# Linear attention and a feed-forward layer on one core: chunks of 384 tokens for 256, TensorE's order pinned, weights decoded without GpSimd

## The chip, the core and the metric

The kernel runs on one core of a Trainium2 chip. The metric is the time of one execution in microseconds (us) on the device; a comparison takes the median of several executions. Five engines work side by side, each through its own instructions in order: TensorE (PE, with its weight loads shown as PEld), VectorE (DVE), ScalarE (ACT), GpSimd (POOL) and SyncE (SP), which here issues the DMA transfers. They meet at semaphores. PE writes into PSUM, which has eight banks of 512 float32 for each of 128 partitions.

## What is computed

```python
def phi(x):                                   # M = 128 random features
    proj = np.einsum('bhsd,md->bhsm', x, omega)
    h = proj - np.sum(x * x, axis=-1, keepdims=True) / 2.0
    h = h - np.max(h, axis=-1, keepdims=True)
    return np.exp(h) / np.sqrt(m)
q_p, k_p = phi(q * scale), phi(k * scale)
kv = np.einsum('bhsm,bhsd->bhmd', k_p, v)
z = np.sum(k_p, axis=2)
num = np.einsum('bhsm,bhmd->bhsd', q_p, kv)
den = np.einsum('bhsm,bhm->bhs', q_p, z)[..., None] + 1e-06
x = (num / den).transpose(0, 2, 1, 3).reshape(B * S, H * D)
h = x @ w_in
out = (h - np.tanh(h)) @ w_out
```

B = 8 batches, H = 8 heads, S = 576 tokens, D = 64; so x has 4608 rows (tokens) of 512. w_in is 512 x 2048 and w_out 2048 x 512. The inputs q, k, v and omega are float32; **both weight matrices arrive as float64**, as pairs of 32-bit words, and the kernel itself turns them into float32.

## The kernel before

**Products.** A float32 product is done on PE in one of two ways. *Native*: one matmul of float32 operands as they are. *Single-pass*: each operand is split into hi (rounded to the type float32r) and lo = x - hi, and the three products hi·hi, hi·lo and lo·hi are added up in PSUM. The feed-forward is single-pass throughout: three matmuls for one.

**Attention.** It works in units of two heads (a head pair, c = 0 to 3). A unit of keys (`k_unit` L156, then `k_single` L202) forms the features of one batch, sums kv (`pk`) and z and spreads z over the partitions (`zb`). A unit of queries (`q_unit` L291) takes 256 tokens: features (L118 single-pass, or `features_f` L139 native with its reductions at L148 and exponentials at L150), denominators on DVE (L322), reciprocal (L325), scaling (L329 on ACT, L331 on DVE or POOL), transposes (L338), numerators (L346 native, L362 and L363 single-pass), and the split into `xh` and `xl`. Each unit is a generator: every `yield` ends a stage, and `tick` (L482) moves all open units by one stage.

**Decoding.** `decode` (L384) takes half a slice of weights (512 words for each partition, 256 for the last four slices) from float64 to hi and lo: ACT L398 and L408, POOL L399 and L409, DVE L400, L402, L405 and L406, and one addition (L410) by turns on POOL and DVE. There are 16 slices of d_ff, each with its part of w_in and of w_out.

**Feed-forward.** Tokens go in 18 chunks of 256. A step takes two slices of d_ff. `ffn_h` (L421) does 24 matmuls 256 wide (L428) into one bank, by turns `h0` and `h1`; ACT takes the tanh (L432), DVE subtracts it from h (L433), ACT rounds to `gh` (L434), and L435 forms `gl`. `ffn_out` (L438) does 12 matmuls 512 wide into `po0` and `po1` (L445 to L447), one step behind, and `ffn_store` (L449) copies out a finished chunk.

**Order of work.** At the start, the keys of batch 0 and the queries of chunks 0 and 1 go natively, while the first weights come. Then, for each of eight steps, two slices are decoded and chunks 0 and 1 are worked off with them (loop at L527), with the native keys of batch 1 and queries of chunks 2 and 3 between. From then on one chunk at a time is done with all weights in SBUF, and a table of start times (L572 to L581) lets a query unit start every four half steps and a key unit where its batch is needed. A scheduler then orders the instructions of every engine by its own estimates, PE's too.

## Time and profile before

| | |
|---|---|
| median of 3 executions | 1107.24 us (1106.55 to 1107.78) |
| span of the profiled execution | 1105.4 us |
| PE, PEld | 1063.0 us (96%), 966.1 us (87%) |
| DVE | 900.0 us (81%) |
| ACT | 703.7 us (64%) |
| POOL | 403.1 us (36%) |
| HBM read, written | 45.15 MB, 9.44 MB |

The profile is that of one execution. The page gives the busy time of each engine over the span; queries of the trace give the same for stretches of time, for groups of equal instructions (count, busy time, mean duration of one, and what ended the idle time before them), and for single instructions in order of time. Matmuls are pipelined: the duration of one overlaps the next, so what a matmul costs is read from start to start.

### The profile page before, as it was taken

Reading aid. Unit: us, or ns where it says so; the run is one execution under the profiler, and the core shown is the slowest. Engines: PE = TensorE matmul, PEld = TensorE weight load, DVE = VectorE, ACT = ScalarE, POOL = GpSimd, SP = SyncE. Lnnn points to the kernel's source line nnn. Section 1 sums busy time; section 2 is a strip of 40 time slices with the busy share of each in tenths; the row PEclk is TensorE's granted clock in tenths of the full one; section 3 lists DMA queues with packets and bytes.
Section 4 is the critical chain, followed back from the end, with each engine's and each line's share of the span. In section 5 each row is a group of like instructions: output and inputs, shape, how many; then the busy total and the mean of one; then the engine's idle time right before and its main releaser. Section 6 shows DMA issues by size and latency. Waiting matters only on the chain. (4 is left out here: it accounts for less than half of the span.)

```text
span 1105.4 us, 21115 instructions
## 1 busy us (share of the span) xinstructions
PE 1063.0 (96%) x6968; PEld 966.1 (87%) x6968; DVE 900.0 (81%) x3079; ACT 703.7 (64%) x1850; POOL 403.1 (36%) x659
## 2 busy tenths in 40 slices
PE   9797888799999999999999999999999999999998
PEld 7577677689989999999999999899999999999997
DVE  5989999989999888678888888998888888666522
ACT  6654445577677776567776776677777766556421
POOL 2787677635553331023333333343333333000000
PEclk9989889999999999999999999999999999999999
DMA  8233312221111111101111111111111110000000
GB/s 232 95 117 99 117 65 96 65 69 31 60 32 51 32 51 32 34 11 51 32 51 29 51 32 51 32 52 32 52 32 51 32 36 15 30 10 25 1 20 20
DMA packets 39244, 55.94 MB, mean 51 GB/s; under 512 B 12896, under 2 KB 22240, under 8 KB 39136
## 3 DMA queue, kind: packets, MB, share of 16 engines
q1 hardware_dynamic: 39056, 54.57, 15.9%
q8 instruction: 55, 0.90, 0.3%
q14 instruction: 53, 0.43, 0.1%
q10 hardware_dynamic: 80, 0.03, 0.0%
HBM read 45.15 MB, written 9.44 MB: 49 GB/s over the span
## 5 line engine op out<-in xcount | busy, mean ns | idle before, releaser
L428 PE MATMUL h<-xh,wih 128*128 128x256 f32 x1152 | 331.0, 288 | 7.7 <-DVE g L433 7.5
L428 PE MATMUL h<-xh,wil 128*128 128x256 f32 x1152 | 329.9, 287 | 2.2 <-DVE wil L410 1.9
L428 PE MATMUL h<-xl,wih 128*128 128x256 f32 x1152 | 329.9, 286 | 0.0
L428 PEld LDWEIGHTS h<-xh,wih 128*128 128x128 f32 x1152 | 221.0, 192 | 14.9 <-issue 5.5
L428 PEld LDWEIGHTS h<-xl,wih 128*128 128x128 f32 x1152 | 221.3, 192 | 4.6 <-issue 0.8
L428 PEld LDWEIGHTS h<-xh,wil 128*128 128x128 f32 x1152 | 221.2, 192 | 3.5 <-DVE wil L410 2.4
L445 PE MATMUL po<-woh,gh 128*128 128x512 f32 x544 | 214.2, 394 | 0.0
L446 PE MATMUL po<-wol,gh 128*128 128x512 f32 x544 | 214.0, 393 | 0.0
L447 PE MATMUL po<-woh,gl 128*128 128x512 f32 x544 | 211.9, 391 | 0.0
L433 DVE TENSOR_TENSOR g<-h,g 128x512 f32<-128x512 f32 x144 | 98.8, 686 | 59.8 <-ACT g L432 58.9
L434 ACT CAST gh<-g 128x512 fp32r<-128x512 f32 x144 | 89.4, 621 | 86.0 <-DVE g L433 83.0
L432 ACT ACTIVATE g<-h 128x512 f32<-128x512 f32 x144 | 85.2, 592 | 87.6 <-PE h L428 79.2
L435 DVE TENSOR_TENSOR gl<-g,gh 128x512 fp32r<-128x512 f32 x128 | 99.7, 779 | 37.8 <-ACT gh L434 36.2
L447 PEld LDWEIGHTS po<-woh,gl 128*128 128x128 f32 x544 | 102.3, 188 | 21.0 <-DVE gl L435 0.4
L445 PEld LDWEIGHTS po<-woh,gh 128*128 128x128 f32 x544 | 102.7, 189 | 16.2
L446 PEld LDWEIGHTS po<-wol,gh 128*128 128x128 f32 x544 | 102.7, 189 | 14.9
L322 DVE CUSTOM_DVE_ANT_0 junk<-phi_q,zb 128x128 f32<-128x128 f32 (+1 forms) x320 | 101.8, 321 | 13.8 <-ACT zb L285 0.4
L225 POOL TENSOR_TENSOR khl<-phi_ka,khl 128x256 fp32r<-128x256 f32 x48 | 38.2, 801 | 116.9 <-DVE khl L224 109.8
L136 ACT ACTIVATE phi_q<-phi_q,nb_q 128x128 f32<-128x128 f32 x232 | 75.7, 391 | 2.5 <-DVE nb_q L132 2.2
L233 POOL CAST vhl<-v 128x128 fp32r<-128x128 f32 (+1 forms) x144 | 45.2, 315 | 85.2 <-PE pk L241 73.8
L356 DVE TENSOR_TENSOR ql<-pt,qh 128x512 fp32r<-128x512 f32 x64 | 43.9, 686 | 29.6 <-ACT qh L355 29.3
L338 PE MATMUL pt<-ident,phi_q 128*128 128x128 f32 x288 | 50.0, 279 | 11.2 <-DVE xs L369 3.8
(152 smaller groups left out, 2198.6 us busy)
## 6 DMA issues: line engine op xcount, KB each, us to landing
kf<-kT SPq DMA_DIRECT2D x32, 288.0 KB, 2.9
qf<-qT SPq DMA_DIRECT2D x72, 128.0 KB, 2.1
out<-o SPq DMA_DIRECT2D x36, 256.0 KB, 2.0
v<-vt SPq DMA_DIRECT2D x24, 288.0 KB, 2.8
raw_i<-w_in SPq DMA_DIRECT2D x12, 512.0 KB, 3.9
raw_o<-w_out SPq DMA_DIRECT2D x12, 512.0 KB, 3.3
v<-va SPq DMA_DIRECT2D x16, 128.0 KB, 3.6
raw_i<-w_in SPq DMA_DIRECT2D x8, 256.0 KB, 2.8
```

The lines of the kernel that those rows point to most:

```text
L136: nc.scalar.activation(ph[:, j], ph[:, j], AF.Exp, bias=nb[:, j : j + 1], scale=-1.0)
L233: nc.gpsimd.tensor_copy(u[p, i, 0], v[p, j])
L322: nc.vector.tensor_tensor_reduce(bank("junk")[r], ph[r, i], kvs[b, c][1][r, h], scale=1.0, scalar=EPS, op0=ALU.mult, op1=ALU.add, accum_ou ...
L338: nc.tensor.transpose(pt[:, i * P : (i + 1) * P], ph[:, ix(i // 2, i % 2)], ident)
L428: nc.tensor.matmul(p[:, j], w, x, start=i == 0, stop=i == len(prods) - 1)
L432: nc.scalar.activation(g, p, AF.Tanh)
L433: nc.vector.tensor_sub(g, p, g)
L434: nc.scalar.copy(gh, g)
L435: mode["gl"].tensor_sub(gl, g, gh.bitcast(F32))
L445: nc.tensor.matmul(po[t], h, woh[f], start=first, stop=False)
L446: nc.tensor.matmul(po[t], h, wol[f], start=False, stop=False)
L447: nc.tensor.matmul(po[t], l, woh[f], start=False, stop=last)
```

## The change

- **Chunks** are 512 tokens, then 256, then ten of 384: twelve in all. A query unit after the start takes 384 tokens, with stages of other lengths.
- **A step** takes one slice of d_ff: 12 matmuls for h, as wide as the chunk, into *one* bank, and three output matmuls for each 128 tokens, first those of gh for all tiles, then those of gl. There are 16 steps a chunk.
- **PSUM**: one bank for h, one for `pk`, three for `po`, and three that projections, transposes and numerators share.
- **The start**: all native attention (keys of batches 0 and 1 and of two pairs of batch 2, queries of the first 768 tokens) and seven decoded slices stand ahead of the first h. Nine slices are decoded beside chunk 0. One transfer of 1 MB fetches a slice, and the order of the first loads on SP is kept as written.
- **Decoding** takes a whole slice at once (1024 words for each partition) in nine steps, three on ACT and six on DVE: none on POOL. It uses other bit operations to the same end.
- **After the decoding**, every matmul and transpose keeps its place in program order (`keep_in_program_order`); the other engines are still ordered by the scheduler. The scalings go half to DVE and half to ACT, where ACT had a quarter.
- **Stores** go in halves of 256 columns, copied by ACT and DVE in turn.

The core of the diff:

```diff
-NS = NF // 2
-TC = 256
+TQ = 256
+TC = 384
+CHUNKS = [(0, 2 * TQ), (2 * TQ, TQ)] + [(t, TC) for t in range(3 * TQ, NT, TC)]
...
+    def mm(*operands, **flags):
+        i = nc.tensor.matmul(*operands, **flags)
+        if mode.get("order"):
+            tc.keep_in_program_order(i)
...
-        nc.scalar.activation(af, topf, AF.Copy, scale=2.0**111)
-        nc.gpsimd.tensor_scalar(af, af, 2.0**-112, 2.0**-111, op0=ALU.mult, op1=ALU.mult)
-        nc.vector.tensor_scalar(a, a, 3, 0x7FFFFFFF, ...)
-        nc.vector.scalar_tensor_tensor(out=top, in0=top, scalar=0x80000000, in1=a, ...)
-        nc.vector.tensor_scalar(a, top, 0xFF800000, None, op0=ALU.bitwise_and)
-        nc.vector.scalar_tensor_tensor(out=af, in0=mid, scalar=2.0**-36, in1=af, ...)
-        nc.scalar.copy(hi, topf)
-        nc.gpsimd.tensor_sub(topf, topf, hi.bitcast(F32))
-        add.tensor_add(lo, topf, af)
+        nc.scalar.activation(a.bitcast(F32), topf, AF.Abs)
+        nc.scalar.activation(m, mid, AF.Copy, scale=128.0)
+        nc.vector.tensor_scalar(a.bitcast(F32), a.bitcast(F32), 2.0**-15, 122879.9921875, ...)
+        nc.vector.tensor_scalar(a, a, 3, 0x3FFFF000, ...)
+        nc.vector.scalar_tensor_tensor(out=a, in0=top, scalar=0xC0000000, in1=a, ...)
+        nc.scalar.copy(hi, a.bitcast(F32))
+        nc.vector.scalar_tensor_tensor(out=m, in0=top, scalar=23, in1=m, ...)
+        nc.vector.tensor_scalar(p, a, 0xFF800000, None, op0=ALU.bitwise_and)
+        nc.vector.scalar_tensor_tensor(out=lo, in0=m, scalar=2.0**-43, in1=p.bitcast(F32), ...)
...
-        p = ps.tile([P, 2, TC], F32, tag=bank("h"), name=f"h_{ch}_{s}")
+        p = ps.tile([P, 512], F32, tag="h", name=f"h_{n}_{s}")[:, :length]
+        prods = [(wt[s][:, i, c * P : (c + 1) * P], x[:, c, r]) for c in range(NC)
+                 for i, x in ((0, xh), (0, xl), (1, xh))]
+        for i, (w_, x) in enumerate(prods):
+            mm(p, w_, x, start=i == 0, stop=i == len(prods) - 1)
...
-        mode["gl"].tensor_sub(gl, g, gh.bitcast(F32))
+        nc.vector.tensor_sub(gl, g, gh.bitcast(F32))
...
+        for t, p in enumerate(po[n]):
+            mm(p, gh[:, tok[t]], wt[s][:, 0, DM:], start=first, stop=False)
+            mm(p, gh[:, tok[t]], wt[s][:, 1, DM:], start=False, stop=False)
+            if last:
+                mm(p, gl[:, tok[t]], wt[s][:, 0, DM:], start=False, stop=True)
+        if not last:
+            for t, p in enumerate(po[n]):
+                mm(p, gl[:, tok[t]], wt[s][:, 0, DM:], start=False, stop=False)
...
+        if decoded < len(wt) and (t >= 5 * decoded + 3 or t >= 26):
+            decode(decoded)
+            decoded += 1
+            if decoded + 1 < NF:
+                fetch(decoded + 1)
+        if len(wt) == NF and done + 2 < decoded and t >= 26:
+            ffn_step(0, done)
+            done += 1
...
+        order=True, chain=False, native=False, norm=[nc.vector, nc.scalar], junk=[junk],
```

Three places in the instructions' order show what moved. The first is PE where the feed-forward begins. Names end in numbers of buffers; `h_0_0` is h of chunk 0, step 0, `pt` and `pn` are the transposes and numerators of queries, `pk` the sums of keys. Before:

```order
L338 MATMUL pt_1_1_508<-ident_64,phi_q1_1_456 128x128 x4
L428 MATMUL h_0_0_705<-xh_0_343,wih0_101 128x256
L428 MATMUL h_0_0_705<-xl_0_344,wih0_101 128x256
L428 MATMUL h_0_0_705<-xh_0_343,wil0_102 128x256
L428 MATMUL h_0_0_705<-xh_0_343,wih0_101 128x256
L338 MATMUL pt_0_2_515<-ident_64,phi_q0_2_476 128x128 x4
L428 MATMUL h_0_0_705<-xl_0_344,wih0_101 128x256
L428 MATMUL h_0_0_705<-xh_0_343,wil0_102 128x256
L346 MATMUL pn_1_1_530<-qt_1_1_513,kvf1_132 128x256 x2
L346 MATMUL pn_0_2_535<-qt_0_2_520,kvf2_133 128x256 x2
```

There the first h is mixed with the queries of head pairs 2 and 3 of chunks 0 and 1 (`pt_0_2`, `pt_1_2`) and the keys of batch 1. The same place after:

```order
L97 MATMUL pk_2_0_1032<-ident_64,z_2_0_1062 128x128 x2
L97 MATMUL pt_2_2_1038<-ident_64,phi_q2_2_996 128x128 x4
L97 MATMUL pk_2_1_1107<-ident_64,z_2_1_1138 128x128 x2
L92 MATMUL pn_2_2_1067<-qt_2_2_1043,kvf02_117 128x64 x2
L92 MATMUL pn_2_2_1067<-qt_2_2_1043,kvf12_125 128x192 x2
L97 MATMUL pt_2_3_1113<-ident_64,phi_q2_3_1081 128x128 x3
L92 MATMUL h_0_0_1179<-xh_98,w0_103 128x512
L92 MATMUL h_0_0_1179<-xl_99,w0_103 128x512
L92 MATMUL h_0_0_1179<-xh_98,w0_103 128x512 x2
L92 MATMUL h_0_0_1179<-xl_99,w0_103 128x512
L92 MATMUL h_0_0_1179<-xh_98,w0_103 128x512 x2
L97 MATMUL pt_2_3_1113<-ident_64,phi_q2_3_1081 128x128
```

Now h begins when only one transpose of the very last query unit (`pt_2_3`, tokens 512 to 767, head pair 3) and its numerators are left of the native attention. In the changed kernel all matmuls have L92 and all transposes L97, the lines of the two helpers.

The second place is DVE between the first feed-forward steps, where decoding (`a`, `raw`, `m` and `w` with the number of the slice) stands between the subtractions that make g. Before:

```order
L433 TENSOR_TENSOR g_0_0_730<-h_0_0_705,g_0_0_730 128x512
L410 TENSOR_TENSOR wol3_116<-raw_o3_0_828,a_o3_0_830 128x512
L148 TENSOR_REDUCE nb_k2_1_1_934<-pj_k2_1_1_935 128x4
L400 TENSOR_SCALAR a_i4_0_1022<-a_i4_0_1022 128x512
L402 SCALAR_TENSOR_TENSOR raw_i4_0_1020<-raw_i4_0_1020,a_i4_0_1022 128x512
L405 TENSOR_SCALAR a_i4_0_1022<-raw_i4_0_1020 128x512
L406 SCALAR_TENSOR_TENSOR a_i4_0_1022<-raw_i4_0_1020,a_i4_0_1022 128x512
L400 TENSOR_SCALAR a_o4_0_1034<-a_o4_0_1034 128x512
L433 TENSOR_TENSOR g_1_0_772<-h_1_0_747,g_1_0_772 128x512
L402 SCALAR_TENSOR_TENSOR raw_o4_0_1032<-raw_o4_0_1032,a_o4_0_1034 128x512
```

Two chunks take turns (`g_0_0`, `g_1_0`), with six steps of decoding, of 512 columns each, between them. After:

```order
L512 TENSOR_TENSOR g_0_0_1194<-h_0_0_1179,g_0_0_1194 128x512
L514 TENSOR_TENSOR gl_0_0_1193<-g_0_0_1194,gh_0_0_1192 128x512
L481 TENSOR_SCALAR a7_1248<-a7_1248 128x1024
L483 TENSOR_SCALAR a7_1248<-a7_1248 128x1024
L488 SCALAR_TENSOR_TENSOR m7_1249<-raw7_1174,m7_1249 128x1024
L512 TENSOR_TENSOR g_0_1_1227<-h_0_1_1212,g_0_1_1227 128x512
L484 SCALAR_TENSOR_TENSOR a7_1248<-raw7_1174,a7_1248 128x1024
L481 TENSOR_SCALAR a8_1293<-a8_1293 128x1024
L514 TENSOR_TENSOR gl_0_1_1226<-g_0_1_1227,gh_0_1_1225 128x512
L490 TENSOR_SCALAR raw7_1174<-a7_1248 128x1024
```

One chunk has its steps one after the other, `gl` is formed here and not on POOL, and the six steps of decoding shown have 1024 columns each.

The third place is PE in the steady stage, in a stretch with a key unit and a query unit open. Before, in chunk 10, step 4 (two slices a step):

```order
L428 MATMUL h_10_4_9374<-xh_10_8206,wil9_1006 128x256
L338 MATMUL pt_11_2_9356<-ident_64,phi_q11_2_9219 128x128 x3
L241 MATMUL pk_5_3_9056<-khl_5_3_5_9320,vhl_5_3_5_9321 128x256 x2
L338 MATMUL pt_11_2_9356<-ident_64,phi_q11_2_9219 128x128
L428 MATMUL h_10_4_9374<-xh_10_8206,wih9_1005 128x256
L428 MATMUL h_10_4_9374<-xl_10_8207,wih9_1005 128x256
L428 MATMUL h_10_4_9374<-xh_10_8206,wil9_1006 128x256
L428 MATMUL h_10_4_9374<-xh_10_8206,wih9_1005 128x256
L428 MATMUL h_10_4_9374<-xl_10_8207,wih9_1005 128x256
L428 MATMUL h_10_4_9374<-xh_10_8206,wil9_1006 128x256
L428 MATMUL h_10_4_9374<-xh_10_8206,wih9_1005 128x256
L241 MATMUL pk_5_3_9056<-khl_5_3_7_9326,vhl_5_3_7_9327 128x256 x2
```

The scheduler set transposes and key sums among the products of one h. After, in chunk 5, at the border of steps 5 and 6:

```order
L92 MATMUL pj_q6_2_1_6766<-om_89,qx_6_2_6686 128x256 x2
L92 MATMUL po0_5_6484<-w4_107,gh_5_4_6641 128x512 x2
L92 MATMUL po1_5_6485<-w4_107,gh_5_4_6641 128x512 x2
L92 MATMUL po2_5_6486<-w4_107,gh_5_4_6641 128x512 x2
L92 MATMUL po0_5_6484<-w4_107,gl_5_4_6642 128x512
L92 MATMUL po1_5_6485<-w4_107,gl_5_4_6642 128x512
L92 MATMUL po2_5_6486<-w4_107,gl_5_4_6642 128x512
L92 MATMUL pj_k5_0_5_6793<-om_89,kxb_5_0_6683 128x256 x2
L92 MATMUL pk_5_0_6801<-khl_5_0_0_6707,vhl_5_0_0_6708 128x256 x2
L92 MATMUL pk_5_0_6801<-khl_5_0_2_6756,vhl_5_0_2_6757 128x256 x2
L92 MATMUL pj_q6_2_2_6816<-om_89,qx_6_2_6686 128x256 x2
L92 MATMUL h_5_6_6829<-xh_98,w6_109 128x384
```

Here everything of the attention stands ahead of or behind the products of h and of the output, none among them: what lies between one h and the next is `po` of the step before and these few.

690 lines of the change are left out of this document (353 added, 337 removed).

## Prediction

> **What bounds the kernel now.** The page comes first: TensorE (PE) is busy for 96% of the span, VectorE (DVE) for 81%.
>
> ```profile
> span 1105.4 us, 21115 instructions
> PE 1063.0 (96%) x6968; PEld 966.1 (87%) x6968; DVE 900.0 (81%) x3079; ACT 703.7 (64%) x1850; POOL 403.1 (36%) x659
> ```
>
> A share of the whole span hides stages, so the second view is the table by stretches of time (start and end, length, busy time of PE, PEld, DVE, ACT and POOL, granted clock, DMA share, GB/s).
>
> ```profile
> 6.00:40.00 34.00, 32.06 (x178) 25.37 (x177) 26.34 (x77) 26.02 (x91) 13.22 (x20) 1.00 0.73 216
> 40.00:80.00 40.00, 32.19 (x168) 26.89 (x167) 36.89 (x83) 23.28 (x59) 33.24 (x39) 0.83 0.29 100
> 80.00:160.00 80.00, 64.84 (x345) 54.64 (x345) 77.61 (x98) 34.62 (x75) 58.37 (x45) 0.89 0.28 92
> 160.00:240.00 80.00, 69.00 (x431) 59.97 (x430) 71.97 (x200) 48.41 (x126) 48.35 (x68) 1.00 0.25 82
> 240.00:560.00 320.00, 319.19 (x2182) 295.44 (x2182) 274.36 (x1062) 225.42 (x602) 112.44 (x212) 1.00 0.13 39
> 560.00:880.00 320.00, 319.51 (x2192) 296.35 (x2192) 279.07 (x1093) 231.82 (x625) 114.95 (x224) 1.00 0.14 41
> ```
>
> There are two kernels in one. From 240 us on PE never stops: 319.19 of 320 us. Before that the weights are decoded, DVE is the full engine (36.89 of 40, 77.61 of 80), and PE idles 7.8, 15.2 and 11.0 us in three rows, partly at a lower clock. So the timeline of PE, at a native projection, at the first feed-forward product and in the late stage, gives the price of a matmul from start to start (the second column, a duration, overlaps the next).
>
> ```profile
> 7.86 1.10 PE L146 MATMUL pj_k<-om_bd,kf 128*128 128x256 f32 x4 [0.38 <-DMA kf<-kT]
> ...
> 47.17 0.36 PE L428 MATMUL h<-xh,wih 128*128 128x256 f32 x1
> ...
> 600.48 0.28 PE L428 MATMUL h<-xh,wih 128*128 128x256 f32 x1
> 600.60 0.28 PE L428 MATMUL h<-xl,wih 128*128 128x256 f32 x1
> 600.72 0.28 PE L428 MATMUL h<-xh,wil 128*128 128x256 f32 x1
> ...
> 601.43 0.38 PE L338 MATMUL pt<-ident,phi_q 128*128 128x128 f32 x2
> 601.57 0.37 PE L428 MATMUL h<-xh,wih 128*128 128x256 f32 x1
> ...
> 603.64 0.40 PE L445 MATMUL po<-woh,gh 128*128 128x512 f32 x1
> 603.87 0.40 PE L446 MATMUL po<-wol,gh 128*128 128x512 f32 x1
> ```
>
> A matmul 256 wide costs 0.120 us, one 512 wide 0.230, a transpose 0.07; a native projection about twice 0.120 (four in some 0.9 to 1.1). The first product of the feed-forward stands at 47 us.
>
> **PE's stream.** The feed-forward of before, 3456 x 0.120 = 415 us for h and 1728 x 0.230 = 397 for the output, is 812 us. After, h is 192 matmuls 512 wide (44 us), 192 of 256 (23) and 1920 of 384. No row shows 384. The nearest rows lie on both sides; a straight line between them gives 0.175, so 336 us. If the cost is all by columns it is 0.1725 (three quarters of 0.230); if nothing of the fixed part is saved, 0.180 (one and a half of 0.120). I take 0.175, half way between its neighbours: h is 403, a gain of 12 us; at 0.180 (and 0.240 for 512 wide) it is nothing. The 1728 output matmuls stay 512 wide. The rows put the fixed part at 0.010 us a matmul. The Trainium skill, "TensorE: Matmul & The Clock Gate", section "Back-to-back issue gap", speaks against this edit: it gives columns over 2.4 GHz plus about 2.5 ns, hence only about 3 us saved by 1152 fewer matmuls. The trace differs, 120 ns where that formula has 109 at 256 columns, and I go by the rows.
>
> The attention that stays behind the first h is 702 matmuls of 256 columns (84 us), 112 of 384 (20), 100 narrower ones at no more than 0.12 (12) and 285 transposes at 0.07 to 0.08 (with what stands between them), so 23: 139 us. Before it was, counted the same way, 896 of some 256 columns (108), 192 narrower ones (22), 328 transposes (26) and 38 native ones at 0.22 (8): 164 us. The native ones, and some of the rest, now lie ahead of the first h. **The stream behind the first h is 403 + 397 + 139 = 939 us, call it 941 with the 2 us that PE idles over such a length** (0.8 and 0.5 us in two rows of 320).
>
> **The start.** All native attention now stands ahead of the first h: 10 units of keys and 12 of queries, where before two batches were spread over 215 us of decoding. On DVE the same stretch also holds seven slices of decoding. The groups of before that price it (busy time, mean ns of one; the last two are ACT's):
>
> ```profile
> L148 DVE TENSOR_REDUCE nb_k<-pj_k 128x4 f32<-128x512 f32 x16 | 10.9, 684 | 5.3 <-PE pj_k L146 5.3
> L148 DVE TENSOR_REDUCE nb_k<-pj_k 64x2 f32<-64x256 f32 x8 | 3.3, 407 | 0.7 <-PE pj_k L146 0.7
> L331 DVE TENSOR_SCALAR phi_q<-phi_q,dn 128x128 f32<-128x128 f32 x177 | 47.8, 325 | 1.0
> L349 DVE TENSOR_TENSOR xl<-pn,xh 128x256 fp32r<-128x256 f32 x8 | 3.2, 414 | 1.2 <-ACT xh L348 1.2
> L400 DVE TENSOR_SCALAR a_i<-a_i 128x512 uint32<-128x512 uint32 x12 | 12.8, 1067 | 1.5 <-POOL a_i L399 1.5
> L405 DVE TENSOR_SCALAR a_i<-raw_i 128x512 uint32<-128x512 uint32 x12 | 5.2, 434 | 0.2
> L405 DVE TENSOR_SCALAR a_i<-raw_i 128x256 uint32<-128x256 uint32 x8 | 2.3, 309 | 0.0
> L402 DVE SCALAR_TENSOR_TENSOR raw_i<-raw_i,a_i 128x512 uint32<-128x512 uint32 x12 | 10.4, 865 | 0.2
> L402 DVE SCALAR_TENSOR_TENSOR raw_i<-raw_i,a_i 128x256 uint32<-128x256 uint32 x8 | 3.6, 464 | 0.0
> L433 DVE TENSOR_TENSOR g<-h,g 128x512 f32<-128x512 f32 x144 | 98.8, 686 | 59.8 <-ACT g L432 58.9
> L398 ACT ACTIVATE a_i<-raw_i 128x512 f32<-128x512 f32 x12 | 8.3, 691 | 4.2 <-DVE a_o L400 2.7 <-DMA raw_i<-w_in 1.4
> L150 ACT ACTIVATE phi_k<-pj_k,nb_k 128x128 f32<-128x128 f32 x64 | 18.3, 384 | 7.7 <-DVE nb_k L148 7.7
> ```
>
> And two denominators from DVE's timeline, 0.21 apart:
>
> ```profile
> 19.77 0.28 DVE L322 CUSTOM_DVE_ANT_0 junk<-phi_q,zb 128x128 f32<-128x128 f32 x1
> 19.98 0.28 DVE L322 CUSTOM_DVE_ANT_0 junk<-phi_q,zb 128x128 f32<-128x128 f32 x1
> ```
>
> Two equal-sized TENSOR_SCALARs, 1067 and 434 ns, show that decoding beside POOL is slow; the changed decoding has no POOL. So I price it by the quiet rows: TENSOR_SCALAR goes from 309 to 434 per 256 columns more, hence 0.684 us at 1024; the two-input form from 464 (256 columns) to 686 (the same engine's product at 512), hence 1.13 at 1024. A slice is three of each, **5.4 us**; by the 512-column rows doubled (2.13, 0.87 and twice that of 865 and more) it would be 10. I take the quiet end and keep 8.0, half way, for a rival.
>
> DVE before the first g: 32 wide reductions x 0.684 = 22, 10 small x 0.407 = 4, 56 denominators x 0.21 = 12, 24 scalings x 0.325 = 8, 12 xl x 0.414 = 5, seven slices 38, and some 5 of reciprocals and small copies: 94 us. The first reduction stands at 6.08 us before; the fetch of the first slice (1 MB) now stands ahead of the first keys on SP's queue, and 1 MB at the 216 GB/s of the second row is nearly 5 us if all went through one after the other, so 6 to 10: I take 7.5. DVE was busy 0.77 of the stretch 6 to 40 and 0.92 of 40 to 80, when decoding filled its gaps. At 0.86 the first h stands at 7.5 + 94/0.86 = **117 us**; at 0.95, 106; at 0.77, 130. ACT's work there (148 exponentials x 0.384 = 57, and seven slices of three steps at twice 0.691 = 29: 86 us) and PE's (74 projections at 0.24 = 18, the rest about 50) lie beside it.
>
> **Chunk 0.** Nine slices are still to be decoded. A step takes PE 12 x 0.230 + 12 x 0.230 = 5.5 us and DVE 5.4 + 0.69 + 0.69 = 6.8: over some six steps until decoding is out of the way 1.3 each, **8 us** (3 if the first slices lie in gaps, 23 at 8.0 us a slice).
>
> **One bank for h.** Now h of a step cannot start before DVE has read the h of the step before. The end of the trace, where no attention is left, shows how long that takes with idle engines:
>
> ```profile
> 1067.81 0.28 PE L428 MATMUL h<-xh,wil 128*128 128x256 f32 x1
> 1068.13 0.60 ACT L432 ACTIVATE g<-h 128x512 f32<-128x512 f32 x1 [3.66 <-PE h L428]
> 1068.77 0.69 DVE L433 TENSOR_TENSOR g<-h,g 128x512 f32<-128x512 f32 x1 [3.57 <-ACT g L432]
> ```
>
> From the last product's end (1068.09) to g's end (1069.46) 1.37 us. PE covers that with the nine output matmuls of the step before, 2.07 us, and whatever attention is pinned there, 0.85 on average. So an idle DVE costs nothing, and a queue of two or three of its instructions ahead of g is late. Before, with two banks, the waits view has little of it (us in total, times, longest):
>
> ```profile
> PE h L428 <- DVE g L433: 7.5, 4, 4.0
> ```
>
> DVE in the steady stage does 274 us per 320. A chunk of 256 tokens is 192 x 0.120 + 96 x 0.230 = 45 us and some 11 of attention, 56 in all, so 48 of DVE; hence 72 per 384 tokens, less 2 for the scalings that move to ACT: 70, against 81 of PE (67 and a tenth of 139). Behind a waiting g stand the attention's own DVE steps, and since PE is pinned, their consumers wait too. I take 0.1 us a step over the 128 steps of chunks 2 to 9, **12 us**, and for chunk 1, with only six output matmuls (1.38 us) over the wait, 0.3 a step, **5**. Bounds: nothing, since the cover is longer than the idle chain, and 45 for both, at three times this.
>
> **The end.** The last matmul is followed by copy and store, 4.1 us:
>
> ```profile
> 1101.28 0.39 PE L447 MATMUL po<-woh,gl 128*128 128x512 f32 x1
> ```
>
> Stores in halves on two engines change that by under 0.5; **4**. Other edits (fewer constants, one fetch per slice) hide beside these.
>
> **Sum:** 117 + 941 + 8 + 5 + 12 + 4 = 1087 of span; the span of before was 1105.4 where the median is 1107.24, so 1.8 lies outside: **1089 us**, a gain of 18. In short: the first h comes 70 us later, but the 78 us that PE lost behind it (1101 - 47, less a stream of 415 + 397 + 164) shrink to 27, the stream loses 12 by width and 25 by what moved ahead.
>
> **Rivals.** First, **slower: DVE and the one bank set the step.** If the queue ahead of g is longer, each step loses 0.3 us and not 0.1: 128 x 0.2 = 26 more, 1115. It decides from 0.14 more a step, where the gain of 18 is gone. For it: DVE at 86% of a PE that may no longer slip another matmul in. Against: PE waited for g only four times before. Chance 0.20. Second, **the start stays long**: the decoding costs 8.0 a slice without POOL too, seven slices before the first h give 18/0.86 = 21 more and chunk 0 gives 15 more, 1125. For it: the 512-column rows; against: the 256-column ones, taken with less POOL. A slower clock would go with it: 0.83 and 0.89 were granted while PE idled a fifth. The Trainium skill, "TensorE: Matmul & The Clock Gate", section "What's actually happening", has the clock halve after an idle window of about 3.4 us; the trace agrees in direction, and by it gaps in the start would cost PE, which has over 40 us to spare there. Chance 0.12. Third, **a packed start**: DVE at 0.95 (106), chunk 0 at 3, chunk 1 at 2, steady 5: 106 + 941 + 3 + 2 + 5 + 4 + 1.8 = 1063. Chance 0.13. Fourth, **384 columns save nothing fixed**: 0.180 each, 1920 x 0.005 = 10 and 2 more on the 512-wide ones: 1101. The rows of before, with no width between 256 and 512, cannot exclude it. Chance 0.08. The Trainium skill's formula quoted above ("TensorE: Matmul & The Clock Gate", "Back-to-back issue gap") leads nearly here.
>
> **The numbers.** My own case has 0.47. What a measurement of this kernel can tell from no change is about 0.2%, 2.2 us. Mine is faster, so is the third; the fourth lies 6 below before, faster, or the same with a few us more of waits; with a little of mine the same: faster 0.63, same 0.05, slower 0.32 (first and second). The range goes from the packed start, 1063, to the long one, 1125.
>
> **What would show it.** Right: first h near 117 us with DVE over 85% busy until then; h 384 wide 0.175 apart; DVE's two-input decode steps at 1.1 us; PE idle of about 0.1 us a step in front of h, released by DVE's g. Wrong: PE idle above 0.25 us in front of each h (first rival), decode steps over 1.5 us or a first h behind 135 (second), 0.180 apart (fourth), a first h before 108 (third).

## The result and the profile after

The changed kernel takes 1137.66 us (median of 4, 1133.69 to 1140.17), the kernel before 1107.22 on the same chips: a ratio of 1.0272, 95% interval 1.0248 to 1.0297. It is slower by 30 us where 18 less were forecast. The page of the changed kernel:

```profile
span 1131.9 us, 18589 instructions
PE 1059.4 (94%) x5722; PEld 942.7 (83%) x5722; DVE 857.7 (76%) x3079; ACT 732.3 (65%) x1918; POOL 259.0 (23%) x572
PEclk8998999999999999999999999999999999999999
```

VectorE and GpSimd have less work than before, TensorE has 4 us less, ScalarE 29 more at a share of only 65%, and the span is 26 us longer. So no busy engine became fuller, and somebody waits. The stretches of the changed kernel, cut where the first h of chunks 0, 1, 2 and 10 stands (columns as in the prediction):

```profile
6.00:100.90 94.90, 87.75 (x470) 69.19 (x471) 85.89 (x258) 75.13 (x223) 11.26 (x24) 0.94 0.56 168
101.00:201.50 100.50, 93.42 (x404) 74.74 (x403) 78.10 (x128) 55.54 (x84) 1.71 (x3) 0.99 0.26 87
201.50:267.00 65.50, 56.98 (x375) 50.91 (x374) 54.12 (x229) 48.98 (x138) 12.65 (x26) 1.00 0.12 36
267.00:984.00 717.00, 674.14 (x3725) 614.47 (x3724) 575.71 (x2278) 494.55 (x1342) 229.72 (x499) 0.99 0.12 35
```

Chunks 2 to 9, the last row, are 3072 tokens. Before, twelve chunks of 256 are as many, from the first h of one chunk to that of another:

```profile
276.00:953.00 677.00, 675.57 (x4620) 625.68 (x4619) 579.90 (x2267) 477.87 (x1281) 230.20 (x441) 1.00 0.13 38
```

This pair says most. Every engine is busy about as long for the same tokens (TensorE 674 and 676 us, VectorE 576 and 580, GpSimd 230 and 230; ScalarE 17 more), yet the changed kernel takes 40 us longer. Before, TensorE idles 1.4 us in 677; after, 43 in 717. The start is not to blame: the first 768 tokens are through at 267 us, where before they took until 276. What TensorE waits for, over the whole run (us in total, times, longest):

```profile
PE h L92 <- DVE g L512: 33.8, 24, 2.9
PE pt L97 <- DVE phq L354: 14.1, 9, 2.3
PE pj_k L92 <- DMA kf<-kT: 5.0, 2, 3.0
PE pk L92 <- ACT zb L324: 4.9, 5, 1.1
PE pj_q L92 <- DVE tmp L435: 2.1, 3, 0.9
```

Of the 33.8 us, 12.2 lie in chunks 0 and 1. In the stage of 717 us the two largest are (the last columns are the idle time before the group and what ended it)

```profile
L92 PE MATMUL h<-xh,w 128*128 128x384 f32 x1024 | 290.0, 344 | 21.6 <-DVE g L512 21.6
L97 PE MATMUL pt<-ident,phq 128*128 128x128 f32 x192 | 33.5, 276 | 12.5 <-DVE phq L354 11.6 <-ACT g L511 0.9
```

so half of the 43 idle us is h waiting for g, and more than a quarter is transposes waiting, nearly all for scaled features; both are VectorE's to deliver. One of the 24, on TensorE in chunk 5: the key sums are done, h of step 6 waits.

```profile
575.17 0.84 PE L92 MATMUL po<-w,gl 128*128 128x512 f32 x3
575.85 0.39 PE L92 MATMUL pk<-khl,vhl 128*128 128x256 f32 x2
578.16 0.44 PE L92 MATMUL h<-xh,w 128*128 128x384 f32 x1 [1.91 <-DVE g L512]
```

And the same moment on ScalarE (the tanh) and VectorE:

```profile
574.74 0.47 ACT L511 ACTIVATE g<-h 128x384 f32<-128x384 f32 x1
...
574.61 0.84 DVE L140 TENSOR_TENSOR qx<-qf,qx 64x384 fp32r<-64x384 f32 x1
575.48 0.29 DVE L261 TENSOR_TENSOR vhl<-v,vhl 128x128 fp32r<-128x128 f32 x1
575.69 0.16 DVE L408 RECIPROCAL dn<-dn 128x2 f32<-128x2 f32 x1
575.88 0.55 DVE L143 TENSOR_TENSOR qx<-qf,qx 64x384 fp32r<-64x384 f32 x1
576.46 0.29 DVE L251 CAST khl<-phk 128x256 fp32r<-128x256 f32 x1
576.67 0.29 DVE L345 CUSTOM_DVE_ANT_0 junk<-phq,zb 128x128 f32<-128x128 f32 x1
576.88 0.76 DVE L354 TENSOR_SCALAR phq<-phq,dn 128x128 f32<-128x128 f32 x1
577.56 0.55 DVE L512 TENSOR_TENSOR g<-h,g 128x384 f32<-128x384 f32 x1
```

The tanh is done at 575.21; g starts at 577.56, since seven steps of a key unit and a query unit stand ahead of it on VectorE (the first of them under way when the tanh ends), without a gap.

Such queues were there before as well. Taken over all steps of the two rows above, from the timelines of ScalarE and VectorE, g starts 0.59 us after the end of its tanh on average in the kernel before (96 steps; 2.86 at most, 26 over 1 us) and 0.49 in the changed one (128 steps; 2.35 at most, 25 over 1 us). So VectorE did not become later with g. What stands over the wait became less.

Where TensorE waits longest, a second price follows:

```profile
400.28 0.62 PE L92 MATMUL h<-xh,w 128*128 128x384 f32 x1 [2.86 <-DVE g L512]
400.70 0.52 PE L92 MATMUL h<-xl,w 128*128 128x384 f32 x1
401.02 0.84 PE L92 MATMUL h<-xh,w 128*128 128x384 f32 x2
...
307.45 0.44 PE L92 MATMUL h<-xh,w 128*128 128x384 f32 x1 [1.91 <-DVE g L512]
...
308.27 0.52 PE L92 MATMUL h<-xl,w 128*128 128x384 f32 x1
308.59 0.84 PE L92 MATMUL h<-xh,w 128*128 128x384 f32 x2
...
578.44 0.34 PE L92 MATMUL h<-xl,w 128*128 128x384 f32 x1
578.62 0.52 PE L92 MATMUL h<-xh,w 128*128 128x384 f32 x2
578.98 0.34 PE L92 MATMUL h<-xl,w 128*128 128x384 f32 x1
```

Behind the wait of 2.86 us the products stand 0.32 us apart, behind that of 1.91 us at 578 us 0.175 to 0.18: the full price. The slow ones last some 3.4 us, and the clock granted meanwhile (400.38 to 403.79 us) is 0.50. The length of one wait does not decide it: another wait of 1.91 us, at 307 us, is followed by products 0.32 apart. There are four such stretches in the 717 us, behind waits of 1.91, 2.46, 2.82 and 2.86 us, and none behind three waits of 2.24 and 2.25. Each costs at most half of its length, all four some 7 us. The Trainium skill ("TensorE: Matmul & The Clock Gate", section "What's actually happening") has the clock halved after an idle window of about 3.4 us that runs freely; the trace agrees with the halving, and shows it after waits that are shorter.

### The profile page after: what moved, and what is told of

Same layout as the page of the kernel before. It is cut to its first block, busy times and chain, and to the rows that moved or that the text cites. A ratio compares the mean times of both kernels' runs of the same rounds, so it can differ in the third digit from the quotient of the medians.

```text
span 1131.9 us, 18589 instructions
## 1 busy us (share of the span) xinstructions
PE 1059.4 (94%) x5722; PEld 942.7 (83%) x5722; DVE 857.7 (76%) x3079; ACT 732.3 (65%) x1918; POOL 259.0 (23%) x572
## 4 chain that ended last, share of the span: by engine, by line
PE 57%; DVE 23%; ACT 10%; DMA 6%; issue 3%; POOL 0%; SPq 0%; DVEq 0%; ACTq 0%; POOLq 0%
PE h L92 25%; PE po L92 22%; DMA raw<-w 3%; DVE junk L345 3%; PE pk L92 2%; PE pt L97 2%; PE pn L92 2%; DMA kf<-kT 2%; DVE gl L514 2%; DVE g L512 2%; PE pj_q L92 2%; DVE phq L154 1%; DVE vhl L261 1%; PE pj_k L92 1%; DMA out<-o 1%
## 5 line engine op out<-in xcount | busy, mean ns | idle before, releaser
L92 PE MATMUL h<-xh,w 128*128 128x384 f32 (+2 forms) x1536 | 431.3, 344 | 33.8 <-DVE g L512 33.8
L92 PEld LDWEIGHTS h<-xh,w 128*128 128x128 f32 x1536 | 283.1, 190 | 51.4 <-DVE g L512 44.0
L92 PE MATMUL po<-w,gh 128*128 128x512 f32 x1152 | 305.4, 397 | 2.5 <-DVE o L83 1.5
L92 PE MATMUL h<-xl,w 128*128 128x384 f32 (+2 forms) x768 | 262.1, 341 | 0.0
L92 PEld LDWEIGHTS po<-w,gh 128*128 128x128 f32 x1152 | 206.5, 189 | 37.4 <-ACT phq L152 1.9
L512 DVE TENSOR_TENSOR g<-h,g 128x384 f32<-128x384 f32 (+2 forms) x192 | 106.3, 554 | 122.5 <-ACT g L511 121.3
L92 PE MATMUL po<-w,gl 128*128 128x512 f32 x576 | 166.4, 390 | 0.0
L92 PEld LDWEIGHTS h<-xl,w 128*128 128x128 f32 x768 | 146.5, 191 | 4.1
L92 PEld LDWEIGHTS po<-w,gl 128*128 128x128 f32 x576 | 108.1, 188 | 23.8 <-DVE gl L514 0.2
L514 DVE TENSOR_TENSOR gl<-g,gh 128x384 fp32r<-128x384 f32 (+2 forms) x192 | 110.0, 573 | 16.0 <-ACT gh L513 13.9
L158 ACT ACTIVATE phk<-phk,nk 128x128 f32<-128x128 f32 x198 | 70.1, 396 | 15.6 <-DVE nk L154 13.4
L97 PE MATMUL pt<-ident,phq 128*128 128x128 f32 x240 | 42.0, 276 | 15.0 <-DVE phq L354 14.1
```

The costliest lines, as they stand in the source:

```text
L92: i = nc.tensor.matmul(*operands, **flags)
L97: i = nc.tensor.transpose(*operands)
L158: nc.scalar.activation(ph[:, i], ph[:, i], AF.Exp, bias=nb[:, i : i + 1], scale=-1.0)
L512: nc.vector.tensor_sub(g, p, g)
L514: nc.vector.tensor_sub(gl, g, gh.bitcast(F32))
```

## The experiments

At the start there were three theories. **A**: h has one bank, and VectorE is late with g. **B**: the pinned places on TensorE cost, since it can't do something else meanwhile. **C**: VectorE has too much to do, wherever the banks are. Of runs without an interval there is one time each; the kernel before lay between 1105.8 and 1107.7 in their company. The changed kernel's own four times lie 6.5 us apart, and its trace is of the fastest, so a single time within some 7 us of 1137.66 tells little. For such runs *the stage* helps: the time from the first g after 768 tokens to the first g after 3840 tokens, in the traces. It is 676 us before and 717 in the changed kernel.

**Not pinned.**

```diff
-        order=True, chain=False, native=False, norm=[nc.vector, nc.scalar], junk=[junk],
+        order=False, chain=False, native=False, norm=[nc.vector, nc.scalar], junk=[junk],
```

> The changed kernel with its matmuls not pinned after the decoding: the scheduler orders TensorE again, still with one bank for h. Theory A (one bank, and on VectorE a queue of attention steps ahead of g): h still waits for g, so PE's waits in front of h stay at 20 us or more and the time falls by 15 us at most, to 1122 or more. Theory B (the pinned places): PE finds other work while g is late, so the 74 us of lost time between 210 and 960 us fall under 30 and the time to 1095 or less. Theory C (VectorE has more work in some steps than TensorE, wherever things stand): the waits are spread out, 1110 to 1130.

1151.92 us, 14 slower than pinned. B falls for this kernel, and C's range (1110 to 1130) is exceeded. A holds in its waits (24.2 us in front of h for g) and in "1122 or more", though nothing in it said that the time would rise. The stage takes 733 us:

```profile
266.00:999.00 733.00, 694.40 (x3732) 623.73 (x3731) 590.36 (x2269) 496.98 (x1343) 241.85 (x499) 0.97 0.12 35
```

TensorE does find other work, as B says: it idles 39 us here and 43 when pinned. But the granted clock is 0.97 and not 0.99. As an estimate, that accounts for at most 15 of the 16 us (0.03 x 733 less 0.01 x 717).

**Two banks for h, and the base with two shared banks.**

```diff
-        p = ps.tile([P, 512], F32, tag="h", name=f"h_{n}_{s}")[:, :length]
+        p = ps.tile([P, 512], F32, tag="h", name=f"h_{n}_{s}", bufs=2)[:, :length]
...
-        pj = ps.tile([P, 2, 2 * M], F32, tag="a", name=f"pj_{name}", bufs=3)
+        pj = ps.tile([P, 2, 2 * M], F32, tag="a", name=f"pj_{name}", bufs=2)
```

> The changed kernel with two PSUM banks for h, taken from the three that projections, transposes and numerators share (two are left). Theory A: the waits in front of h (33 us) go, and with the next run as its base the time is 25 to 40 us less. Theory B: PE's other pinned places still wait (transposes and key sums), so the gain is under 15. Theory C: the wait moves from h to the transposes, under 15 as well, with the waits for the attention's steps up by as much as those for g go down.

> The changed kernel with two shared banks and not three, one bank of PSUM left unused: the base for the run with two banks for h. All theories: 0 to 15 us more than the changed kernel, 1133 to 1150, by how often three of projections, transposes and numerators are open at once.

The second pair of lines stands for all tiles with the tag "a"; the base has only that one. 1147.16 with two banks for h, 1155.10 with one (5 more than the base was given), both with two shared; the stage takes 731 and 739 us. With two for h, TensorE's waits are:

```profile
PE pt L97 <- DVE phq L354: 16.4, 12, 2.3
PE pj_q L92 <- DVE tmp L435: 16.1, 9, 2.9
PE pj_k L92 <- DVE tmp L435: 13.9, 15, 1.3
...
PE h L92 <- DVE g L512: 2.2, 2, 1.7
```

And in the base:

```profile
PE h L92 <- DVE g L512: 18.5, 17, 1.7
PE pj_q L92 <- DVE tmp L435: 16.1, 9, 2.9
PE pj_k L92 <- DVE tmp L435: 14.2, 16, 1.3
PE pt L97 <- DVE phq L354: 9.2, 6, 2.2
```

The waits for g are gone, 16 us of them, and it brings 8 us and not 25, as B and C had it (under 15): 7 us come back in front of transposes, the next pinned matmuls that need VectorE. The projections' waits are the base's; they come with the two shared banks. A has the first wait right and not the loss.

**Without denominators** (left out: the sums of features times z after the start).

```diff
-            for h in range(2):
-                den(dn, 2 * t + h, ph[:, t, h], pieces, t, h, c)
+            nc.gpsimd.memset(dn[:, 2 * t : 2 * t + 2], 1.0)
```

> The changed kernel without the denominators of the query units after the start (264 steps of VectorE, about 55 us, are left out; the scaling takes ones). Everything else stays: one bank, pinned matmuls. Theory A and C: the queue ahead of g is shorter by 5.5 us a chunk, and most of the waits go: 1085 to 1105. Theory B, by which the places on TensorE are what costs: under 15 us, 1120 or more.

1100.85 us, 37 less. VectorE's busy time falls by 73.5 us, by the pages (857.7 and 784.2), where 55 were expected. The stage of chunks 2 to 9 takes 681 us:

```profile
271.00:952.00 681.00, 663.54 (x3725) 608.42 (x3724) 514.41 (x1834) 491.10 (x1343) 230.41 (x586) 1.00 0.13 37
```

So VectorE's work is on the path, although it is busy only 80% of that stage in the changed kernel: g now starts 0.17 us after its tanh on average, and not 0.49. But this run also takes a link out of each query unit's chain, from the exponentials to the scaling, and the transposes' waits go with it. The next two leave that link in.

**One step of the key unit on GpSimd.** In the changed kernel VectorE's largest wait in total that isn't for the tanh is:

```profile
DVE zhl L308 <- PE pk L92: 28.3, 16, 3.0
```

```diff
-        nc.vector.tensor_copy(zhl[:, 0], zs)
+        nc.gpsimd.tensor_copy(zhl[:, 0], zs)
```

> The changed kernel with one step of the key unit, the rounding of its sum z (zhl, 22 times), on GpSimd and not on VectorE. In the trace of the changed kernel VectorE stands 28 us idle at this step, since its buffer is read by key matmuls that TensorE reaches later than the scheduler assumed, and g is queued behind it. Theory D (VectorE's order is right for a TensorE that runs on time, and where TensorE runs late, VectorE blocks itself): that idle time goes and 15 to 30 us of the time, 1105 to 1122. Theory C (the sum of VectorE's work alone): 8 us of work are gone, so 4 to 8 us, 1128 to 1134.

1130.68 us, 7 less by the time and within what single runs differ by; the stage takes 715 us, 2 less. D falls: VectorE's 28 us of waiting there were not the loss (TensorE still waits 32.3 us for g).

**Less work of other kinds.**

```diff
-                nc.vector.tensor_sub(u[p, i, 1], v[p, j], u[p, i, 0].bitcast(F32))
+                nc.gpsimd.tensor_sub(u[p, i, 1], v[p, j], u[p, i, 0].bitcast(F32))
-        order=True, chain=False, native=False, norm=[nc.vector, nc.scalar], junk=[junk],
+        order=True, chain=False, native=False, norm=[nc.scalar], junk=[junk],
```

> The changed kernel with 154 subtractions for the lower part of v on GpSimd (about 47 us of VectorE's time) and all scalings of queries on ScalarE (another 34 us). Theory C: as when the denominators were left out (55 us less work gave 37), so 35 to 55 us less, 1083 to 1102. If it is a question of single waits (theory D) rather than of the sum: 15 us or less, and ScalarE or GpSimd become what PE waits for.

1118.08 us, 20 less, which neither C (35 to 55) nor D (15 or less) had. VectorE's busy time falls by 53 us, by the pages (857.7 and 804.6), and not by the 81 expected; ScalarE has 29 more and GpSimd 58. TensorE's waits in front of transposes went (14.1 us, now under 1.1), those for g hardly (30.0 us). So most of the gain comes by the scalings, it seems, which no longer stand in VectorE's queue; the two edits were not tried apart. At the rate of the run without denominators (37 for 73.5) 53 us would have given 27: this run does not decide between the sum of VectorE's work and its single late steps.

**Keys further apart.**

```diff
-            last = min(last - 10, first[n, c] - 12)
+            last = min(last - 12, first[n, c] - 12)
```

> The changed kernel with a key unit started every 12 half steps and not every 10, so that fewer stages of keys fall on the same step as stages of queries. If bursts of VectorE's work are what makes g late, the largest waits (steps 6 and 15 of the chunks, 2 to 3 us each) shrink, and the time falls by 10 to 25 us, 1112 to 1128. If it is the sum of the work, it stays within 8 us of 1137.7.

1139.72 us: no gain. The stage takes 712 us, 5 less, but it begins 11 us later (5 of them already at the first g, where runs with the same start differ by up to 7), since the keys now begin earlier. The longest wait for g is 2.9 us as before, and in the stage these waits are more (33.6 us): other steps are late instead.

**The kernel before with the change's parts, one by one.** Pinned from the third chunk on:

```diff
-    mode.update(pj=["pj0", "pj1"], pk=["pk"], pt=["pt"])
+    mode.update(pj=["pj0", "pj1"], pk=["pk"], pt=["pt"], order=True)
```

> The kernel before (256 tokens, two banks for h, two slices a step) with its matmuls and transposes pinned to program order from the third chunk on. If a pinned TensorE is what costs (theory B), this is slower by 15 us or more, 1120 and up. If pinning does little and the rest of the change costs (theories A and C): within 10 us of before, 1098 to 1115.

Its matmuls and transposes go through the two helpers of the changed kernel. 1182.83 us, 76 slower. The largest wait of TensorE is for the lower parts of keys, which GpSimd makes, in front of key sums (26.7 us in 46 waits): the stages of before were not laid out to be executed as written. With one bank for h:

```diff
-    mode.update(pj=["pj0", "pj1"], pk=["pk"], pt=["pt"])
+    mode.update(pj=["pj0", "pj1"], pk=["pk"], pt=["pt"], h=["h0"])
```

> The kernel before with one bank for h in place of two from the third chunk on, everything else as it was, TensorE not pinned. Theory A (the second bank of h is what kept PE fed): PE waits for g in most steps and the time rises by 30 us or more, over 1135. Theory C (work and bursts of VectorE, wherever the bank): under 15 us, since the output matmuls and the attention stand over the wait; 1105 to 1120.

1113.36 us, 6 slower, 4 of them in the stage (680 us). In the steady stage TensorE still hardly stops:

```profile
280.00:904.00 624.00, 621.39 (x4238) 573.71 (x4238) 544.99 (x2091) 446.01 (x1184) 215.06 (x413) 1.00 0.13 39
```

VectorE is 87% busy there, more than in the changed kernel, with one bank, and TensorE idles 2.6 us. That ends A and C as they stood. Its g is as late as ever, 0.55 us behind the tanh on average. A step of before has 12 output matmuls (2.76 us) and 1.4 us of attention over the wait for g, the changed one 9 and 0.85. So, theory **E**: the short step. One slice of d_ff a step in the kernel before, with two banks and with one:

```diff
-        for s in range(NS):
+        for f in range(NF):
...
-            g = ffn_h(ch, s, *x_of[ch])
+            g = one_h(ch, f, *x_of[ch])
...
-                ffn_out(*prev)
+                one_out(*prev)
```

`one_h` does the 12 products of one slice and its g, `one_out` six output matmuls, and one stage of the attention follows each step.

> The kernel before with one slice of d_ff a step from the third chunk on: 12 products of h, then 6 output matmuls, with the attention's stages as often per slice as before; two banks for h, not pinned. Theory E (what lets g be late without a wait is the work that stands over it, and the change made that short): two banks still leave a whole h of 1.4 us and the output over g, so little is lost; the narrower instructions of VectorE cost 0.3 us per 7 us on an engine that is 86% busy. 1107 to 1125. Theory F (smaller steps are bad in themselves, more instructions and hand-overs per token): 1140 or more.

> The same with one bank for h. Theory E: now only 1.4 us of output and some 0.7 of attention stand over g, which before came 2.5 us behind the end of h on average: 0.5 to 1 us a step over 256 steps, 100 us or more on top of the run with two banks, 1200 or more. Theory F: like the run with two banks within 15 us.

1158.10 and 1187.53 us: the short step costs 51, the one bank on top of it 29, where it cost 6 with the long step; 39 and 24 of that lie in the stage (715 and 739 us). TensorE's waits for g are 10.8 us in 20 waits with two banks and 29.9 in 46 with one. For the first run F's forecast (1140 or more) came true and not E's; for the second neither did (100 more by E, 15 by F). So the one bank costs little more than its waits (19 us more), but most of what the short step costs with two banks is not the wait for g, and stays open. Part of it may be work: g and gl take VectorE, by the groups of the run with two banks,

```profile
L461 DVE TENSOR_TENSOR gl<-g,gh 128x256 fp32r<-128x256 f32 x256 | 119.1, 465 | 38.9 <-ACT gh L460 33.1 <-PE po L470 3.1 <-PE h L454 1.0
L459 DVE TENSOR_TENSOR g<-h,g 128x256 f32<-128x256 f32 x256 | 107.7, 421 | 90.8 <-ACT g L458 88.7 <-issue 0.2
```

227 us in 256 pairs of 256 columns, where 128 pairs of 512 took about 187 (128 x (686 + 779) ns, by the page of before); this part the changed kernel does not have.

**Both, not pinned and with two banks**, in the changed kernel and with chunks of 256 tokens (one slice a step, pinned and not):

```diff
-TC = 384
+TC = 256
```

With 256 tokens the third output tile's bank goes to h. It is also taken from the projections of the start: in the two runs with 256 tokens here and the three of the next part the first g stands at 131 to 142 us and not at 107, and 10 to 27 us are lost by the time that 768 tokens are through.

> The changed kernel not pinned and with two banks for h (two shared banks): both parts of the suspicion at once, to be read against the unpinned one with one bank (1151.9) and the pinned one with two (1147.2). Theory A: unpinned, a second bank lets PE go on while g is late, 1100 to 1125. Theory C: it stays above 1135, since the attention's steps then wait for VectorE.

> The changed kernel with chunks of 256 tokens behind the first 768, pinned, one slice a step, and the bank that the third output tile took given to h (two for h, three shared). TensorE's stream grows by 11 us for the narrower h and by a few more in the attention. Theory A (the 384 columns cost the second bank of h): the waits go down by more than that, 1100 to 1125. Theory C: VectorE's work per token is the same or higher (more instructions), the steps are shorter, and the time rises, 1140 to 1170.

> The kernel with chunks of 256 tokens, two banks for h, three shared banks and one slice a step (1235.5 pinned), now not pinned: like the steady stage of before but for one slice a step. If the pinned places were what cost 100 us there (57 us of waits in front of transposes), it falls to 1120 or less. If one slice a step costs (twice as many steps of g and gl on VectorE, each half as wide, about 0.2 us more for a pair), it stays above 1150.

1243.97, 1235.52 and 1312.14 us: A's forecasts fail, and the times lie far above C's range too where it gave one (1140 to 1170). In none is h's wait for g the largest; the transposes' is (17.8, 60.8 and 30.3 us). The clock granted over the two unpinned runs was 0.921 and 0.915, where the changed kernel had 0.987. In the first of them the stage is

```profile
280.00:1086.00 806.00, 741.02 (x3730) 649.47 (x3730) 591.32 (x2286) 504.19 (x1349) 238.16 (x501) 0.91 0.11 31
```

75 us longer than in the pinned run with two banks (731 us, a granted clock of 0.98). TensorE idles 17 us more than there (65 and 48); the lower clock can account for at most 58 more (0.09 x 806 less 0.02 x 731, an estimate). So most of what this run loses is clock, and it says little about the banks.

**The long step back in the changed kernel**, theory **G**: chunks of 256, two slices a step, two banks, units of 256 tokens. The decoding stays; the start loses a bank, as said above.

```diff
+        p = ps.tile([P, 2, TC], F32, tag="h", name=f"h_{n}_{s}", bufs=2)
+        for j in range(2):
+            f = 2 * s + j
...
-            last = max(last + 7, t0 + 32 * (n - 2) - 10 + 8 * c)
+            last = max(last + 4, t0 + 16 * (n - 2) - 4 + 4 * c)
```

> The changed kernel with the long step of before from chunk 1 on: chunks of 256 tokens, two slices of d_ff a step in one bank, two banks for h, three shared, and units of 256 tokens whose stages are set to half steps of 3.5 us (two extra pauses fewer). Start, decoding and pinned order are the changed kernel's. TensorE's products get 11 us longer. Theory G (short steps with one bank are what loses the 40 us in the steady stage): the loss goes, 1085 to 1110. Theory B again (pinned places: 77 us in the kernel before): it stays at 1135 or more.

> The same, not pinned: the start and decoding of the changed kernel with a steady stage like that of before. Theory G: 1085 to 1110, since before ran this stage without loss, and its first 768 tokens took 9 us more than the changed kernel's. If the new attention units (more shared banks, other stages) are what costs, 1130 or more, as with one slice a step.

Pinned 1243.30 us (ratio 1.1251, interval 1.1215 to 1.1288), not pinned 1219.36 (1.1004, 1.0961 to 1.1047). G fails as a forecast of the time. The waits for g did go, to under 6 us, and the query units' own chain took their place; not pinned:

```profile
PE pt L97 <- DVE phq L354: 33.0, 14, 5.6
PE pt L97 <- ACT phq L352: 12.6, 6, 3.5
PE pn L92 <- ACT qh L422: 3.4, 11, 0.4
```

The same run's stretch from 300 to 1000 us has a granted clock of 0.94 (the column behind GpSimd's):

```profile
300.00:1000.00 700.00, 650.50 (x4131) 588.67 (x4131) 545.99 (x2122) 461.44 (x1270) 213.05 (x466) 0.94 0.12 34
```

A second buffer for the features of a query unit:

```diff
-        qf=(ak, 1), qx=(ak, 1), phq=(ak, 1), qh=(ak, 2), ql=(ak, 2), tmp=(ak, 1), kf=(ak, 1),
+        qf=(ak, 1), qx=(ak, 1), phq=(ak, 2), qh=(ak, 2), ql=(ak, 2), tmp=(ak, 1), kf=(ak, 1),
```

> The run with 256 tokens, two slices a step and no pinning, with two buffers for the features of a query unit and not one (and two, not four, for the copied output, which makes the room). In that run PE waits 46 us for scaled features in front of transposes and hardly for g (6 us). Theory H (units with single buffers follow each other too closely, so their chains of ScalarE, VectorE and TensorE steps stand one behind the other): the waits in front of transposes halve and the time falls by 50 us or more, to 1170 or less. If it is the chain of steps within a unit, the time stays above 1195.

1221.20 us (1.1008, 1.0972 to 1.1044): no difference, and TensorE waits 49.7 us for scaled features where it was 45.6. It isn't that buffer, as far as this shows, since the buffers of the copied output were halved to make room. What remains is the chain within a unit, or the other single buffers; it wasn't taken apart further.

**The decoding alone**, in the kernel before:

```diff
-        nc.scalar.activation(af, topf, AF.Copy, scale=2.0**111)
...
-        nc.gpsimd.tensor_sub(topf, topf, hi.bitcast(F32))
-        add.tensor_add(lo, topf, af)
+        nc.scalar.activation(af, topf, AF.Abs)
+        nc.scalar.activation(m, mid, AF.Copy, scale=128.0)
...
```

The nine new steps are those of the changed kernel, 512 and 256 columns wide.

> The kernel before with the changed decoding alone (three steps on ScalarE, six on VectorE, none on GpSimd, in the pieces of 512 and 256 columns of before, one piece fewer in flight at the end). VectorE's share of a slice was about 9 us before (142 us in 16 slices) and would be 7 with pieces of 512 at the quiet price; the stage before 216 us, in which VectorE is full, shrinks by 15 to 40 us: 1068 to 1093. If the start was bound by the transfers or by TensorE's native work instead, within 8 us of 1107.

1095.79 us, a ratio of 0.990 (0.9883 to 0.9916): faster than both kernels, and just outside the range expected (1068 to 1093). The first h of the third chunk stands at 202 us and not 216, where 15 to 40 less were expected. One slice on VectorE is cheaper, and TensorE gets more done meanwhile, though VectorE is still the full engine:

```profile
80.00:160.00 80.00, 70.62 (x426) 59.68 (x426) 75.04 (x181) 52.73 (x122) 16.01 (x16) 1.00 0.32 102
```

TensorE is busy 70.62 of these 80 us, where it was 64.84 before, and the granted clock is 1.00 where it was 0.89.

## Why the prediction was wrong

Point by point, by its own steps:

- **384 columns**: right. The 1920 products of h stand 0.175 us apart in the median of the trace, as the rows above show, half way between 256 and 512. The Trainium skill's formula of columns over 2.4 GHz plus about 2.5 ns ("TensorE: Matmul & The Clock Gate", "Back-to-back issue gap") gives 0.1625: at full clock the trace differs by 12 ns. In the slow stretch it shows 0.32, as the same section's formula for the cold clock has it, columns over 1.2 GHz.
- **Decoding**: right. The quiet rows gave 0.684 and 1.13 us; it is

```profile
L488 DVE SCALAR_TENSOR_TENSOR m<-raw,m 128x1024 uint32<-128x1024 uint32 x7 | 8.5, 1220 | 0.1
L483 DVE TENSOR_SCALAR a<-a 128x1024 uint32<-128x1024 uint32 x7 | 4.8, 686 | 0.1
```

so 5.7 us a slice and not 5.4. Without GpSimd no step is slow (the longest of all 96 took 1.23 us), so the second rival (a long start) falls.
- **The start**: the first h stands at 101 us, not 117. VectorE's work ahead of it was 86 us where 94 were summed, at a pace of 0.905 where 0.86 was taken. This was the third rival's mechanism, and 16 us better than the forecast. (The 216 GB/s that the prediction took for the first transfer stand in the first row of its table, not the second; the sum is as it should be.)
- **Chunks 0 and 1**: 166 us together, where the prices of the prediction for TensorE (16 x 5.5 and 45, and some 12 of attention by the matmuls that the trace has there) and its 13 us of waits make 158. TensorE idles 15.6 us there, so the waits are about right; 8 us over in all.
- **One bank for h, 0.1 us a step**: this is the step that failed. Chunks 2 to 9 take 717 us. The prediction spread its 139 us of attention evenly over ten chunks; by the matmuls that the trace has, some 120 of them lie in these eight, so that its own prices make 8 x 67 + 120 + 12 = 668. That is 49 us over, 0.38 us more a step. 31 of them are idle time, 43 us where 12 were set: 21.6 for g and 12.5 in front of transposes, the rest in small parts. Some 7 are the stretches at half clock. Another 7 are a price: 234 transposes here, each 0.109 us from the next in the median, where 0.08 was taken. The first rival had the place, the sign and the reason in the trace (a queue of attention steps ahead of g on VectorE, TensorE that can't slip anything in), but priced it at 26 and was given 0.20. Its sign, more than 0.25 us in front of each h, did not show: the waits for g are 0.17 a step, and the transposes' come on top.
- **The end**: chunks 10 and 11 and the last store take 148 us, where its prices make 145. With the start 16 us early and 8, 49 and 3 over, the span of 1132 comes out of the 1087 forecast.
- **How it was mis-sized**: the prediction compared 86% of VectorE with 100% of TensorE and called the rest cover. The average hid two things. First, the step: what stands over the wait for g went from 4.2 us a step of 7 to 2.9 of 5, while g comes as late as ever behind its tanh (0.49 us on average and 2.35 at most, by the count above, where it was 0.59 and 2.86). Second, it argued that PE waited for g only four times before, in a kernel where the second bank let g be late without a wait.
- **Pinning**: was to make consumers wait. In the changed kernel TensorE idles 4 us more with it in the stage, and the kernel still gains 14, which the granted clock (0.99 against 0.97 without) can account for.

**What is shown, and what stays open.** Shown: the loss is in the stage of chunks 2 to 9, at nearly equal busy times; the largest wait is h for g, behind attention steps on VectorE, and VectorE is no later with g than before; with less work on VectorE time comes back; a short step costs the kernel before 51 us, and one bank costs 29 with a short step and 6 with a long one. Not shown: that the short step and the one bank are all of the 40 us, and why the short step costs most of its 51 us with two banks. Where they were undone in the changed kernel, the query units became what TensorE waits for, and the time rose. That the attention's units of the changed kernel (their stages, their single buffers, the shared banks) are tuned to its own half steps is argued from that, no more. 384 tokens with two slices a step weren't tried: g and its parts would need twice their room in SBUF.

## What to carry to other kernels

Judge the cover over a hand-over between engines step by step, against the longest burst that can stand ahead of it, and not by the busy share of a stage: here an engine that is 80% busy held up one at 94%, and one at 87% hardly did. Here the wider tile took a PSUM bank and the step became shorter, so the cover lost twice, in work and in buffers; the gain forecast for the width (12 us) is small beside 0.38 us more on each of 128 steps. And when a change is made of many parts, try its cheapest alone: the decoding was worth 11 us in the kernel before, and the changed kernel with all parts takes 42 us more than that.

## What the runs showed of the hardware

In the changed kernel's stage, half the clock for about 3.4 us of products (0.32 us for 384 columns and not 0.175) followed waits of 1.91 to 2.86 us, but other waits of 1.91 to 2.25 us were followed by the full clock. In runs with more waits these stretches are longer: one of 20.5 us at 0.50 stands at 562 us of the unpinned run with two banks for h. The kernels that took 1219 us and more had a granted clock of 0.915 to 0.967, against 0.987 in the changed kernel. Two-input steps of VectorE, all operands in SBUF, took 1.22 us for 1024 columns where GpSimd does nothing of the decoding; where it does, before, 512 columns took 0.87 to 1.41 on average, by group.
